# Weight loads in pieces, column norms, and a denser interleave in an attention and top-1 MoE kernel

## The chip, the core and the metric

The kernel runs on one core of a Trainium2 chip. A core has five engines that each run their own list of instructions in order: PE (TensorE: matmuls and transposes), DVE (VectorE), ACT (ScalarE), POOL (GpSimd) and SP (SyncE, which here only issues transfers); 16 DMA engines move the data. The metric is the device time of one execution in microseconds (us).

## The reference

Attention over columns, for each of 4 batches of 5056 tokens with 256 channels, and then a mixture of 8 experts of which each of the 20224 tokens uses one:

```python
qn = q / (norm(q, axis=1) + 1e-6);  kn = k / (norm(k, axis=1) + 1e-6)
s = softmax(kn.T @ qn / tau)              # 256 x 256 for each batch
x = v @ s                                 # 5056 x 256 for each batch
e = argmax(x @ w_gate)                    # one expert for each token
g = softmax(x @ w_gate)[e] * sigmoid((x @ w_output_gate)[e])
out[token] = g * (relu(x[token] @ w1[e]) @ w2[e])     # w1 256x1024, w2 1024x256
```

## The kernel before, in words

**Stages.** `gram(b)` makes s for one batch: 20 steps, each with two token rows for each of the 128 partitions, load q and k (SP, tile qk, 6 buffers), square them on ACT (L353), add the squares up on DVE (L354) and multiply on PE (s_ps, L366). Then come the norms: `both` is the sum of squares, PE adds it over the partitions with a matrix of ones (L381 for the norms of q, as a row that stands on every partition; L383 for those of k, as columns), ACT takes the root (L389), DVE does one Newton step and the reciprocal (L390 to L397) and scales s (L401). Softmax, a transpose and the product with the gate weights follow.

`mix(b)` makes x for one batch. It has 5 groups of 1024 tokens; in a group, 4 steps load v (SP, L465), transpose it on PE (vt_ps, L477), split it into a rounded part and a rest (vh on ACT L481, vl on DVE L483) and multiply (x_ps, L506 to L508); ACT copies x into the group's tile `st` (L509). After a group, `route` finds each token's expert on DVE (r_oh, L556), counts on PE (r_ps, L576) and has POOL scatter the tokens to DRAM by expert (xs_d, L598), eight transfers a group.

`blocks` runs the experts in units of 256 or 128 tokens: `fetch_w` has POOL fetch the unit's weights by an index (wbuf, L825), `fetch_x` has SP load its tokens (xg, L843), `prepare` splits these into two f16 parts (xr, ACT L880 and DVE L881) and has SP issue transposing transfers (xt, L885), `h_part` and `y_part` are the matmuls (L919 to L921, L942 to L944), `store` has POOL scatter the result (L954). A token load waits for a **mark**: a small POOL transfer (L615) behind the scatters of the tokens in question.

`prep` and `split` turn an expert's f32 weights into two f16 parts for the ranks 0 to 7 (experts in the order of their token counts so far): two loads of 1 MB (raw, L273 and L276) from the row that a table `ri` gives (SP reads it at L268), two Squares each on ACT for the scale (L297), a sum on PE (w_ps, L301), scaled copies (whi on ACT L310, wlo on DVE L311), and two writes to DRAM (wsc, L316). Rank 0 goes straight into wbuf. The raw of rank 1 lies in the `raw` buffers, that of the ranks above in `st` buffers, which the routing uses too.

**What sets the order.** The functions are generators, and the driver at the end takes steps of them in turn: Gram 0; mix(0) and mix(1) with the Grams 1 to 3 at GRATE (1.3) Gram steps to a mixing step; checkpoint 0 (the ranks); mix(2) with what is left of Gram 3, with the weights of rank 0 at PRATE, and from step OPEN on with the first units of `blocks`; checkpoint 1; mix(3) with blocks at BRATE and the weights of ranks 1 to 7 at MRATE; checkpoint 2; the other blocks with the remaining weights at WRATE. `pause(n)` gives n steps away. A scheduler orders each engine's list within that; each engine then runs its list in order and waits where its operands are late.

## Time and profile before

| | |
|---|---|
| median of 3 runs | 1206.93 us (1206.85 to 1208.63) |
| the profiled execution | 1209.88 us, its span in the trace 1208.1 us |
| mean granted PE clock | 0.990 |
| PE busy | 1174.4 us, 97% of the span |
| DVE, ACT, POOL busy | 748.5, 602.3, 517.9 us |
| mean DMA rate | 173 GB/s |

The profiled execution is one run, 2.95 us above the median. Times in rows of the trace are counted from the start of the span. Gram 0 and the first loads fill about the first 60 us; mix(2) runs to about 300 us, mix(3) to about 420, the units alone from there on. PE matmuls are pipelined: the duration of one is longer than the spacing to the next. Of an f32 matmul with a moving tile of 256 or 1 columns the trace has two records.

### The profile page before, as it was taken

To read this page: it belongs to the slowest core of one execution; us is meant where nothing else is said; L and a number is where in the kernel's file an instruction comes from. 1 tells how busy PE (TensorE), PEld (TensorE's weight loads), DVE (VectorE), ACT (ScalarE), POOL (GpSimd) and SP (SyncE) were. 2 spreads that over 40 slices of the span, in tenths; PEclk is the share of its full clock that TensorE was granted. 3 is DMA by queue.
4 is the path that set the end of the run, shared out by engine and by line. 5 is a ranking of instruction groups with operands and counts; after the bars stand their busy time and mean duration, and the time that the engine had idled before them with its cause. 6 is when DMAs were issued, how large, how long until landed. Compare 5 with 4: busy or idle time off the path is not lost.

```text
span 1208.1 us, 28097 instructions
## 1 busy us (share of the span) xinstructions
PE 1174.4 (97%) x10412; PEld 1066.4 (88%) x10412; DVE 748.5 (62%) x2300; ACT 602.3 (50%) x1193; POOL 517.9 (43%) x518
## 2 busy tenths in 40 slices
PE   8999999997997999999999999999999999999997
PEld 7899999887996888888888888888889999999997
DVE  7787768788685966566666654555554555555531
ACT  6576656576574555555556443333333444344432
POOL 0003756536565753333444433344444444444433
PEclk9999999998998999999999999999999999999999
DMA  9976888877767898657554436643325534336533
GB/s 319 330 246 207 301 277 259 295 242 215 212 242 236 223 264 178 150 147 174 148 137 126 112 80 113 182 76 77 72 63 176 112 73 82 79 81 197 168 104 130
DMA packets 186307, 208.56 MB, mean 173 GB/s; under 512 B 121832, under 2 KB 134510, under 8 KB 182200
## 3 DMA queue, kind: packets, MB, share of 16 engines
q1 hardware_dynamic: 145368, 139.41, 42.0%
q0 software_dynamic: 40512, 67.05, 18.9%
q8 instruction: 84, 1.38, 0.5%
q14 instruction: 55, 0.45, 0.1%
q10 hardware_dynamic: 288, 0.26, 0.1%
HBM read 281.84 MB, written 61.41 MB: 284 GB/s over the span
## 4 chain that ended last, share of the span: by engine, by line
PE 87%; DMA 6%; DVE 2%; issue 2%; ACT 1%; SPq 1%; POOL 0%; POOLq 0%; DVEq 0%; ACTq 0%
PE h_ps L919 11%; PE h_ps L921 11%; PE h_ps L920 11%; PE y_ps L942 11%; PE y_ps L943 11%; PE y_ps L944 11%; PE s_ps L366 10%; PE x_ps L506 3%; PE x_ps L508 2%; PE x_ps L507 2%; PE vt_ps L477 2%; DMA wbuf<-wsc,wi 1%; DMA qk<-in_k_dram 1%; DMA raw<-in_moe_w_dram 1%; DMA qk<-in_q_dram 1%
## 5 line engine op out<-in xcount | busy, mean ns | idle before, releaser
L924 DVE SCALAR_TENSOR_TENSOR hb<-h_ps,hb 128x512 f16<-128x512 f32 (+1 forms) x360 | 228.5, 636 | 276.0 <-ACT hb L923 275.1
L923 ACT ACTIVATE hb<-h_ps 128x512 f16<-128x512 f32 (+1 forms) x360 | 197.9, 552 | 364.1 <-PE h_ps L921 362.5
L919 PE MATMUL h_ps<-xt,wbuf 128*128 128x256 f16 (+1 forms) x1440 | 366.5, 262 | 3.0 <-ACT st L509 3.0
L921 PE MATMUL h_ps<-xt,wbuf 128*128 128x256 f16 (+1 forms) x1440 | 366.6, 262 | 0.0
L920 PE MATMUL h_ps<-xt,wbuf 128*128 128x256 f16 (+1 forms) x1440 | 366.5, 262 | 0.0
L942 PE MATMUL y_ps<-wbuf,hb 128*128 128x256 f16 x1296 | 353.3, 273 | 5.0 <-ACT yo L948 2.4
L944 PE MATMUL y_ps<-wbuf,hb 128*128 128x256 f16 x1296 | 353.3, 273 | 0.0
L943 PE MATMUL y_ps<-wbuf,hb 128*128 128x256 f16 x1296 | 353.3, 273 | 0.0
L825 POOL DMA_INDIRECT wbuf<-wsc,wi x172 | 177.8, 1034 | 404.5 <-PE h_ps L921 365.2
L598 POOL DMA_INDIRECT xs_d<-st,r_si x160 | 168.1, 1051 | 199.2 <-DVE r_d L550 101.9
L954 POOL DMA_INDIRECT out_dram<-yo,b_id x162 | 165.4, 1021 | 69.2 <-issue 42.3
L366 PE MATMUL s_ps<-qk 128*128 128x256 f32 x640 | 152.4, 390 | 5.8 <-DMA qk<-in_q_dram 3.9
L920 PEld LDWEIGHTS <-wbuf 128*128 128x128 f16 x1440 | 141.0, 98 | 16.9 <-issue 3.2
L919 PEld LDWEIGHTS <-wbuf 128*128 128x128 f16 x1440 | 142.1, 99 | 14.1
L921 PEld LDWEIGHTS <-wbuf 128*128 128x128 f16 x1440 | 141.1, 98 | 13.3
L943 PEld LDWEIGHTS <-hb 128*128 128x128 f16 x1296 | 126.8, 98 | 19.3 <-issue 5.6
L366 PEld LDWEIGHTS s_ps<-qk 128*128 128x128 f32 x640 | 121.4, 196 | 21.2 <-DMA qk<-in_k_dram 3.9
L944 PEld LDWEIGHTS <-hb 128*128 128x128 f16 x1296 | 126.8, 98 | 14.9
L942 PEld LDWEIGHTS <-hb 128*128 128x128 f16 x1296 | 126.8, 98 | 14.3
L354 DVE TENSOR_TENSOR acc<-acc,sq 128x1024 f32<-128x1024 f32 x76 | 92.9, 1223 | 46.8 <-ACT sq L353 45.4
L880 ACT ACTIVATE xr<-xg,b_sx 128x256 f16<-128x256 f32 x162 | 74.6, 502 | 66.8 <-DVE b_sx L233 46.4
L353 ACT ACTIVATE sq<-qk 128x1024 f32<-128x1024 f32 x76 | 80.3, 1060 | 53.0 <-DMA qk<-in_k_dram 44.8
(191 smaller groups left out, 1448.8 us busy)
## 6 DMA issues: line engine op xcount, KB each, us to landing
xg<-xs_d SPq DMA_DIRECT2D x72, 272.0 KB
qk<-in_q_dram SPq DMA_DIRECT2D x75, 256.0 KB
qk<-in_k_dram SPq DMA_DIRECT2D x75, 256.0 KB
v<-in_v_dram SPq DMA_DIRECT2D x32, 512.0 KB
raw<-in_moe_w_dram SPq DMA_DIRECT2D x16, 1024.0 KB
wsc<-whi SPq DMA_DIRECT2D x14, 512.0 KB
wsc<-wlo SPq DMA_DIRECT2D x14, 512.0 KB
v<-in_v_dram SPq DMA_DIRECT2D x8, 480.0 KB
```

The lines of the kernel that those rows point to most:

```text
L366: nc.tensor.matmul(s_ps[:, c, :], kt[:, 1, t, c * P : (c + 1) * P], qt[:, 0, t, :], start=st == 0 and t0 == 0 and t == 0 and c == 0 and n ...
L598: ins = nc.gpsimd.indirect_dma_start(out=xs_d[:, :], out_offset=bass.IndirectOffsetOnAxis(ap=si[:np_, t : t + 1], axis=0), in_=st[:np_, t, ...
L825: nc.gpsimd.indirect_dma_start(out=wbuf[half][:, at_of(u), :], out_offset=None, in_=wsc[half][:end, :], in_offset=bass.IndirectOffsetOnAxi ...
L919: nc.tensor.matmul(hp, w1s[:, 0, c, fs], xh, start=fi == 0 and c == 0, stop=False, **KWM)
L920: nc.tensor.matmul(hp, w1s[:, 0, c, fs], xl, start=False, stop=False, **KWM)
L921: nc.tensor.matmul(hp, w1s[:, 1, c, fs], xh, start=False, stop=fin, **KWM)
L923: nc.scalar.activation(hh, h_ps[:, :, :w], AF.Relu)
L924: nc.vector.scalar_tensor_tensor(out=hb[:, 1, 2 * fp : 2 * fp + 2, :w], in0=h_ps[:, :, :w], scalar=0.0, in1=hh, op0=ALU.max, op1=ALU.subtract,
L942: nc.tensor.matmul(y_ps[:, t, :], hb[:, 0, f, tsl], w2s[:, 0, f, :], start=st, stop=False, **KWM)
L943: nc.tensor.matmul(y_ps[:, t, :], hb[:, 0, f, tsl], w2s[:, 1, f, :], start=False, stop=False, **KWM)
L944: nc.tensor.matmul(y_ps[:, t, :], hb[:, 1, f, tsl], w2s[:, 0, f, :], start=False, stop=fin, **KWM)
L954: ins = nc.gpsimd.indirect_dma_start(out=out[:, :], out_offset=bass.IndirectOffsetOnAxis(ap=un["id"][:, t : t + 1], axis=0), in_=un["yo"][ ...
```

## The change

The raw weights are loaded in two halves each, and from rank 2 on into buffers of the tile `v` instead of `st`; each half of the two f16 parts is written to DRAM as soon as it is made, in pieces of 256 KB instead of 512 KB. The norms of q and k are both taken as columns (four matmuls with one column of ones, 128x4 values), with the inverse root on DVE by a shift of the exponent and two Newton steps and a correction, all on 128x4; for q the result is put on the diagonals of two 128x128 matrices (dq), and a further matmul with ones (n_ps) makes the row on every partition; s is scaled from there. ACT's root goes. The Gram rate in mix(0) and mix(1) is 1.45. The preparation of weights has other rates and pauses, its part in mix(3) is cut after rank 1, the blocks open two mixing steps sooner (OPEN 8), and token loads are looked for in every step of a unit.

```diff
-    GRATE = 1.3
-    PRATE = 1.2
-    DEEP, LAG, REST = 2, 3, 2
-    LATE, OPEN, MARKED = 5, 10, 3
+    GRATE, AHEAD_RATE = 1.3, 1.45
+    PRATE = 1.5
+    DEEP, LAG, REST, SLOW = 2, 4, 1, 4
+    LATE, OPEN, MARKED = 5, 8, 3
     FAR, NEAR = 5, 1
     BRATE = 0.7
     DRY = 4
-    MRATE = 1.2
-    WRATE = 0.8
+    MRATE = 1.6
+    WRATE = 1.0
...
-                raw = wk.tile([P, R, CW], F32, tag="st", name=f"raw{r}_{half}", bufs=STB)
-                raw = raw.rearrange("p r w -> p (r w)")[:, :HW1]
+                parts = [
+                    ld.tile([P, 4, C], F32, tag="v", name=f"raw{r}_{half}_{i}", bufs=VB).rearrange("p t c -> p (t c)")
+                    for i in range(2)
+                ]
             else:
                 raw = big.tile([P, HW1], F32, tag="raw", name=f"raw{r}_{half}", bufs=3)
+                parts = [raw[:, i * HW1 // 2 : (i + 1) * HW1 // 2] for i in range(2)]
+            raws.append(parts)
...
+            rows = wraw[half][bass.ds(row, P), :]
+            for i, part in enumerate(parts):
+                if half == 0:
+                    nc.sync.dma_start(part, rows[:, i * HW1 // 2 : (i + 1) * HW1 // 2])
+                else:
+                    nf = FC // 2
+                    of = rows.rearrange("(f a) (b d) -> (a b) f d", f=FC, d=C)[:, i * nf : (i + 1) * nf, :]
+                    nc.sync.dma_start(part.rearrange("p (f d) -> p f d", f=nf), of)
+                yield
...
-                gather()
-                yield
-            yield from pause(LAG if n == 0 else REST)
+                yield from gather()
+            yield from pause(LAG if n == 0 else SLOW if r > AHEAD + 1 else REST)
...
+            for n, part in enumerate((hi, lo)):
+                nc.sync.dma_start(wsc[half][rows, n * HW1 + a.start : n * HW1 + a.stop], part[:, a])
             yield
-        for n, part in enumerate((hi, lo)):
-            nc.sync.dma_start(wsc[half][rows, n * HW1 : (n + 1) * HW1], part)
...
-        nc.tensor.matmul(k_ps[:, :C], onesf, both[:, 0, :], start=True, stop=True, skip_group_check=True)
+        for i in range(2):
+            for c in range(CC):
+                n = i * CC + c
+                nc.tensor.matmul(
+                    k_ps[:, n : n + 1], both[:, i, c * P : (c + 1) * P], onesf[:, 0:1],
+                    start=n == 0, stop=n == 2 * CC - 1, skip_group_check=True,
+                )
...
+        ss, hss, half, y = t4("n_ss"), t4("n_hss"), t4("n_half", I32), t4("n_y")
+        nc.vector.tensor_scalar(out=ss, in0=k_ps[:, : 2 * CC], scalar1=1e-36, scalar2=None, op0=ALU.max)
+        nc.vector.tensor_scalar(
+            out=half, in0=ss.bitcast(I32), scalar1=1, scalar2=None, op0=ALU.logical_shift_right
+        )
+        nc.vector.tensor_scalar(
+            out=y.bitcast(I32), in0=half, scalar1=-1.0, scalar2=float(RSQRT), op0=ALU.mult, op1=ALU.add
+        )
+        nc.vector.tensor_scalar(out=hss, in0=ss, scalar1=-0.5, scalar2=None, op0=ALU.mult)
+        for _ in range(2):
+            t = t4("n_t")
+            nc.vector.tensor_tensor(out=t, in0=hss, in1=y, op=ALU.mult)
+            nc.vector.tensor_tensor(out=t, in0=t, in1=y, op=ALU.mult)
+            nc.vector.scalar_tensor_tensor(out=y, in0=t, scalar=1.5, in1=y, op0=ALU.add, op1=ALU.mult)
+        r, e = t4("n_r"), t4("n_t")
+        nc.vector.tensor_tensor(out=r, in0=ss, in1=y, op=ALU.mult)
+        nc.vector.tensor_tensor(out=e, in0=r, in1=r, op=ALU.mult)
+        nc.vector.tensor_tensor(out=e, in0=ss, in1=e, op=ALU.subtract)
+        nc.vector.scalar_tensor_tensor(out=e, in0=e, scalar=0.5, in1=y, op0=ALU.mult, op1=ALU.mult)
+        nc.vector.scalar_tensor_tensor(out=r, in0=e, scalar=1e-6, in1=r, op0=ALU.add, op1=ALU.add)
+        nc.vector.tensor_scalar(out=r[:, CC:], in0=r[:, CC:], scalar1=tau_b, scalar2=None, op0=ALU.mult)
+        nc.vector.reciprocal(r, r)
+        dq = one.tile([P, CC, P], F32, tag="root", name=f"dq{b}")
         for c in range(CC):
-            nc.tensor.matmul(
-                k_ps[:, C + c : C + c + 1], both[:, 1, c * P : (c + 1) * P], onesf[:, 0:1],
-                start=False, stop=c == CC - 1, skip_group_check=True,
-            )
-        ss = k_ps[:, : C + CC]
-        root = one.tile([P, C + CC], F32, tag="root", name=f"root{b}")
-        nc.scalar.activation(root, ss, AF.Sqrt)
-        nc.vector.tensor_scalar(out=root, in0=root, scalar1=1e-30, scalar2=None, op0=ALU.max)
-        r = one.tile([P, C + CC], F32, tag="rq", name=f"rn{b}")
-        nc.vector.reciprocal(r, root)
-        nc.vector.tensor_tensor(out=r, in0=ss, in1=r, op=ALU.mult)
-        nc.vector.tensor_tensor(out=r, in0=r, in1=root, op=ALU.add)
-        nc.vector.tensor_scalar(out=r, in0=r, scalar1=0.5, scalar2=1e-6, op0=ALU.mult, op1=ALU.add)
-        nc.vector.tensor_scalar(out=r[:, C:], in0=r[:, C:], scalar1=tau_b, scalar2=None, op0=ALU.mult)
-        nc.vector.reciprocal(r, r)
-        yield from pause(HOLD)
-        rq, rk = r[:, :C], r[:, C:]
+            nc.vector.tensor_scalar(out=dq[:, c, :], in0=ident, scalar1=r[:, c : c + 1], scalar2=None, op0=ALU.mult)
+        yield from pause(HOLD + 1)
+        n_ps = ps_x.tile([P, 512], F32, tag="x", name=f"n_ps{b}")
+        nc.tensor.matmul(n_ps[:, :C], onesf, dq.rearrange("p c m -> p (c m)"), start=True, stop=True)
+        yield
+        rq, rk = n_ps[:, :C], r[:, CC:]
...
+                adv("x", fetch_x, got["prep"] + QKB)
...
-        _beside(mix(b) if b else first, (ahead, GRATE))
+        _beside(mix(b) if b else first, (ahead, AHEAD_RATE))
...
-    preps = prep(AHEAD, E)
+    preps = chain(prep(AHEAD, AHEAD + 1), pause(12), prep(AHEAD + 1, E))
```

How this moves the instructions is seen in three places. In the rows, a number behind a name tells tiles of one name apart, and xN counts neighbours that are alike. The first place is ACT around the start of mix(2)'s second group, where the weights of rank 0 (tiles raw_0 and raw_1) are squared; sq are the Gram's squares, st_0 and st_1 the first two groups' tiles. Before:

```order
L353 ACTIVATE sq_15_0_3168<-qk_15_3165 128x1024
L509 COPY st_0_2766<-x_ps 128x272
L481 CAST vh<-vt_ps 128x512
L509 COPY st_1_2954<-x_ps 128x272 x2
L297 ACTIVATE wbuf_155,wss<-raw_0_2793 128x1024 x2
L559 ACTIVATE r_d<-r_d 128x64
L481 CAST vh<-vt_ps 128x512
L567 ACTIVATE r_og_2936<-r_og_2936 128x8
L509 COPY st_1_2954<-x_ps 128x272 x2
L297 ACTIVATE wbuf_156,wss<-raw_1_2833 128x1024 x2
L481 CAST vh<-vt_ps 128x512
L353 ACTIVATE sq_16_0_3246<-qk_16_3243 128x1024
```

And now:

```order
L359 ACTIVATE sq_19_0_3245<-qk_19_3238 128x1024
L537 COPY st_0_2889<-x_ps 128x272 x2
L509 CAST vh<-vt_ps 128x512
L537 COPY st_0_2889<-x_ps 128x272
L304 ACTIVATE wbuf_155,wss<-raw_0_2916 128x1024
L537 COPY st_0_2889<-x_ps 128x272
L304 ACTIVATE wbuf_155,wss<-raw_0_2916 128x1024
L587 ACTIVATE r_d<-r_d 128x64
L304 ACTIVATE wbuf_156,wss<-raw_1_2957 128x1024
L509 CAST vh<-vt_ps 128x512
L595 ACTIVATE r_og_3061<-r_og_3061 128x8
L537 COPY st_1_3079<-x_ps 128x272
```

The Squares of the weights stood as two pairs ahead of the last four steps of Gram 3 (sq_16 is the first of them); now all Gram steps stand before them, and they stand singly between copies of x, vh and the routing.

The second place is the norms of Gram 3, in mix(2). On DVE now, from the first reading of the sums (wbuf is the split of rank 0's weights, r_ names belong to the routing):

```order
L399 TENSOR_SCALAR n_ss_3363<-k_ps_3358 128x4
L582 TENSOR_REDUCE r_mv<-r_val 128x8
L400 TENSOR_SCALAR n_half_3365<-n_ss_3363 128x4
L317 SCALAR_TENSOR_TENSOR wbuf_155<-raw_0_2916,wsw,wbuf_155 128x1024
L584 TENSOR_TENSOR r_oh<-r_val,r_mv 128x64
L406 TENSOR_SCALAR n_hss_3364<-n_ss_3363 128x4
L403 TENSOR_SCALAR n_y_3366<-n_half_3365 128x4
L317 SCALAR_TENSOR_TENSOR wbuf_155<-raw_0_2916,wsw,wbuf_155 128x1024
L592 TENSOR_TENSOR r_os<-st_1_3079,r_oh 128x64
L511 TENSOR_TENSOR vl<-vt_ps,vh 128x512
L409 TENSOR_TENSOR n_t_3371<-n_hss_3364,n_y_3366 128x4
```

and the chain's end, with the diagonals and the scaling of s:

```order
L417 SCALAR_TENSOR_TENSOR n_r_3379<-n_t_3380,n_r_3379 128x4
L418 TENSOR_SCALAR n_r_3379<-n_r_3379,tau_b 128x2
L597 SCALAR_TENSOR_TENSOR r_gt<-r_og_3564,r_se 128x8
L419 RECIPROCAL n_r_3379<-n_r_3379 128x4
L598 RECIPROCAL st_2_3333<-r_gt 128x8
L422 TENSOR_SCALAR dq_3388<-ident,n_r_3379 128x128 x2
L429 SCALAR_TENSOR_TENSOR s_sb_3252<-s_sb_3252,n_r_3379,n_ps_3533 128x256 x2
```

On PE now, between the sums (k_ps) and the new matmul (n_ps), with the alike rows of the mixing left out:

```order
L390 MATMUL k_ps_3358<-onesf,both_3356 128x1 x4
L534 MATMUL x_ps<-ah_2442,vh 128x272
...
L505 MATMUL vt_ps<-ident,v_3_0_3448 128x128 x4
L505 MATMUL vt_ps<-ident,v_3_2_3571 128x128 x4
...
L604 MATMUL r_ps<-r_oh,tri 128x64
...
L505 MATMUL vt_ps<-ident,v_3_2_3571 128x128 x4
L505 MATMUL vt_ps<-ident,v_4_0_3671 128x128 x4
L425 MATMUL n_ps_3533<-dq_3388,onesf 128x256
L308 MATMUL w_ps<-wss,onesf 128x2
L534 MATMUL x_ps<-ah_2442,vh 128x272
```

Before, the norms of q came from one matmul of 256 columns, and there was no second one:

```order
L508 MATMUL x_ps<-ah_2498,vl 128x272
L381 MATMUL k_ps_3521<-both_3519,onesf 128x256
L383 MATMUL k_ps_3521<-onesf,both_3519 128x1 x2
L301 MATMUL w_ps<-wss,onesf 128x2
L477 MATMUL vt_ps<-ident,v_4_0_3546 128x128 x4
L477 MATMUL vt_ps<-ident,v_4_2_3688 128x128 x4
L506 MATMUL x_ps<-ah_2498,vh 128x272
```

Between k_ps and n_ps PE has 36 x matmuls (12 rows of each of the lines 534 to 536), 16 transposes and one group of r_ps; n_ps stands ahead of w_ps and the next x matmuls. On DVE 50 rows lie between n_ss and the scaling of s, of which 17 are the chain's small operations, 4 vl, 2 weight splits and 2 dq.

The third place is ACT in mix(3), where unit 4, the first behind the second mark, is prepared (xr; st_1 and st_2 are groups of mix(3), the pieces of raw_0 and raw_1 belong to rank 1). Before:

```order
L481 CAST vh<-vt_ps 128x512
L509 COPY st_2_4619<-x_ps 128x272 x3
L880 ACTIVATE xr_3657<-xg,b_sx 128x256 x2
L509 COPY st_2_4619<-x_ps 128x272
L297 ACTIVATE whi_1_4850,wss<-raw_1_4164 128x1024 x2
L880 ACTIVATE xr_3657<-xg,b_sx 128x256 x2
L923 ACTIVATE hb<-h_ps 128x512
```

And now:

```order
L537 COPY st_1_4451<-x_ps 128x272
L587 ACTIVATE r_d<-r_d 128x64
L537 COPY st_1_4451<-x_ps 128x272
L595 ACTIVATE r_og_4433<-r_og_4433 128x8
L509 CAST vh<-vt_ps 128x512
L908 ACTIVATE xr_3663<-xg,b_sx 128x256 x2
L537 COPY st_1_4451<-x_ps 128x272
L908 ACTIVATE xr_3663<-xg,b_sx 128x256 x2
L537 COPY st_1_4451<-x_ps 128x272
```

It stood in the middle of group st_2; now it stands after the second copy of group st_1.

More of the change, by code (lines that the diff above doesn't have):

```diff
@@ L24 @@
 EXP_MASK = 0x7F800000
+RSQRT = 0x5F3759DF
 def _beside(main, *others):
@@ L271, in gather @@
             )
-            if half == 0:
-                nc.sync.dma_start(raw, wraw[0][bass.ds(row, P), :])
-            else:
-                rows = wraw[1][bass.ds(row, P), :].rearrange("(f a) (b d) -> (a b) f d", f=FC, d=C)
-                nc.sync.dma_start(raw.rearrange("p (f d) -> p f d", f=FC), rows)
-            raws.append(raw)
+            rows = wraw[half][bass.ds(row, P), :]
[7 more added lines that the diff above has]
+                yield
         for n, (r, half) in enumerate(jobs):
             while len(raws) < min(n + DEEP, len(jobs)):
-                gather()
-                yield
-            yield from pause(LAG if n == 0 else REST)
+                yield from gather()
+            yield from pause(LAG if n == 0 else SLOW if r > AHEAD + 1 else REST)
             yield from split(raws[n], half, r)
@@ L296, in split @@
             a = slice(i * HW1 // 2, (i + 1) * HW1 // 2)
-            nc.scalar.activation(hi[:, a], raw[:, a], AF.Square, accum_out=ss[:, i : i + 1])
+            nc.scalar.activation(hi[:, a], raw[i], AF.Square, accum_out=ss[:, i : i + 1])
             yield
@@ L305, in split @@
         root2(tot, KW, sw, invw[:, half, r : r + 1])
-        src, dh, dl = raw, hi, lo
-        cuts = [(slice(None), slice(i * HW1 // 2, (i + 1) * HW1 // 2)) for i in range(2)]
-        for i, a in enumerate(cuts):
-            nc.scalar.activation(dh[a], src[a], AF.Copy, scale=sw)
+        for i in range(2):
+            a = slice(i * HW1 // 2, (i + 1) * HW1 // 2)
+            nc.scalar.activation(hi[:, a], raw[i], AF.Copy, scale=sw)
             nc.vector.scalar_tensor_tensor(
-                out=dl[a], in0=src[a], scalar=sw, in1=dh[a], op0=ALU.mult, op1=ALU.subtract
+                out=lo[:, a], in0=raw[i], scalar=sw, in1=hi[:, a], op0=ALU.mult, op1=ALU.subtract
             )
+            for n, part in enumerate((hi, lo)):
+                nc.sync.dma_start(wsc[half][rows, n * HW1 + a.start : n * HW1 + a.stop], part[:, a])
             yield
-        for n, part in enumerate((hi, lo)):
-            nc.sync.dma_start(wsc[half][rows, n * HW1 : (n + 1) * HW1], part)
         if half == 1:
@@ L397, in gram, with t4 @@
-        nc.vector.reciprocal(r, r)
-        yield from pause(HOLD)
-        rq, rk = r[:, :C], r[:, C:]
+        for i in range(2):
+            for c in range(CC):
[4 more added lines that the diff above has]
+                )
+        def t4(tag, dt=F32):
+            return sm.tile([P, 2 * CC], dt, tag=tag, name=f"{tag}{b}")
```

## The prediction

> **What bounds the kernel now.** I read first the page's busy shares and the chain that ended last.
>
> ```profile
> PE 1174.4 (97%) x10412; PEld 1066.4 (88%) x10412; DVE 748.5 (62%) x2300; ACT 602.3 (50%) x1193; POOL 517.9 (43%) x518
> PE 87%; DMA 6%; DVE 2%; issue 2%; ACT 1%; SPq 1%; POOL 0%; POOLq 0%; DVEq 0%; ACTq 0%
> ```
>
> TensorE is the bound; an edit can win only what PE loses. So next the stretches (length, then busy time of PE, PEld, DVE, ACT, POOL, then granted clock, DMA share, GB/s), to find where it loses.
>
> ```profile
> 60.00:150.00 90.00, 90.00 (x630) 84.44 (x630) 69.30 (x168) 63.76 (x128) 33.70 (x32) 1.00 0.77 251
> 210.00:300.00 90.00, 78.75 (x561) 73.27 (x560) 70.71 (x268) 56.44 (x126) 44.37 (x46) 0.94 0.80 253
> 360.00:390.00 30.00, 22.44 (x176) 19.92 (x176) 17.00 (x74) 15.05 (x34) 16.04 (x17) 0.89 0.81 247
> 450.00:750.00 300.00, 300.00 (x2757) 269.11 (x2756) 183.94 (x521) 151.17 (x283) 119.25 (x115) 1.00 0.57 138
> 369.30:372.70 3.40, 2.93 (x12) 2.75 (x13) 0.87 (x5) 0.51 (x1) 1.58 (x2) 0.50 1.10 201
> sum 17.00, PE 14.53 PEld 13.01 DVE 7.14 ACT 8.22 POOL 7.64; mean PE 3.63 PEld 3.25 DVE 1.79 ACT 2.06 POOL 1.91
> ```
>
> PE is idle 11.25 us in 210:300 and 7.56 in 360:390, and 1.6 at a weight fetch (the last wait below): 20.4. The last two rows are of the stretches in which the clock stood at 0.50 (four, behind these stops, 17.0 us in all; one is shown, and the sum): 14.53 us of busy time at half clock, of which half, 7.3, is lost. Together **27.7 us** lie in reach. What PE waited for from 200 to 430 us (in total, times, longest):
>
> ```profile
> PE r_ps L576 <- DVE r_oh L556: 5.3, 1, 5.3
> PE r_ps L576 <- ACT st L509: 4.1, 1, 4.1
> PE h_ps L919 <- ACT st L509: 3.0, 1, 3.0
> PE y_ps L942 <- ACT yo L948: 2.4, 1, 2.4
> PE vt_ps L477 <- DVE vl L483: 2.1, 1, 2.1
> PE y_ps L942 <- DMA wbuf<-wsc,wi: 1.6, 1, 1.6
> ```
>
> Each goes back to one cause on another engine. The 4.1 (at 239 us): ACT, in order, stood at the first Square of the first expert's weights; SP had not issued their load sooner because it waited for the table row of the expert.
>
> ```profile
> 239.59 1.06 ACT L297 ACTIVATE wbuf<-raw 128x1024 f16<-128x1024 f32 x1 [7.00 <-DMA raw<-in_moe_w_dram]
> SPq L268 <- DVE tb_ni L666: 6.0, 1, 6.0
> ```
>
> The 5.3 (at 284): DVE's backlog behind the norm chain of the last Gram matrix. PE's norm matmuls, ACT's table load for the root, and DVE (start, length):
>
> ```profile
> 271.43 0.59 PE L381 MATMUL k_ps<-both,onesf 128*128 128x256 f32 x2
> 271.86 0.50 PE L383 MATMUL k_ps<-onesf,both 128*128 128x1 f32 x4
> 272.22 0.36 PE L301 MATMUL w_ps<-wss,onesf 128*128 128x2 f32 x2
> 272.44 1.07 PE L477 MATMUL vt_ps<-ident,v 128*128 128x128 f32 x8
> ...
> 272.74 1.28 ACT L389 ACT_TABLE_LOAD   x1
> ...
> 276.05 1.76 DVE L392 RECIPROCAL rn<-root 128x258 f32<-128x258 f32 x1
> 284.78 1.75 DVE L397 RECIPROCAL rn<-rn 128x258 f32<-128x258 f32 x1
> 288.66 0.20 DVE L561 TENSOR_REDUCE r_se<-r_d 128x8 f32<-128x64 f32 x1
> 288.79 0.21 DVE L556 TENSOR_TENSOR r_oh<-r_val,r_mv 128x64 bf16<-128x64 f32 x1
> ```
>
> From the sums (272.2) to the second reciprocal's end (286.5) go 14.3 us; r_oh, behind it, starts at 288.79. The 3.0, 2.4 and 2.1 (367 to 380): SP stood at a raw load whose buffer, a routing tile, had to be scattered first, and behind it stood the transposes that ACT's xr tiles needed.
>
> ```profile
> SPq L276 <- DMA xs_d<-st,r_si: 18.5, 2, 9.4
> 360.39 9.85 SPq L885 DMA_TRANSPOSE xt<-xr  x4
> 371.62 0.51 ACT L880 ACTIVATE xr<-xg,b_sx 128x256 f16<-128x256 f32 x1 [7.06 <-DMA xt<-xr]
> ```
>
> **Part by part.** *Gram rate 1.45.* The last Gram steps come before the first expert's load, and ACT's Squares of that load are parted by st and vh copies, so the table row and the load have some two groups' PE work as cover. The 4.1 and its clock go; left I take 1 (0 to 4, the whole old stop; SP still can't load before the table row). The denser Gram loads in mix(0) and mix(1) meet DMA engines at 0.77 where PE was 90.00 of 90: nothing, up to 2, none below.
>
> *Norms in columns.* Prices from the groups (busy, mean ns), and the spacing of x matmuls from two neighbours:
>
> ```profile
> L392 DVE RECIPROCAL rn<-root 128x258 f32<-128x258 f32 x4 | 7.0, 1762 | 0.1
> L394 DVE TENSOR_TENSOR rn<-rn,root 128x258 f32<-128x258 f32 x4 | 1.7, 418 | 0.0
> L396 DVE TENSOR_SCALAR rn<-rn,tau_b 128x2 f32<-128x2 f32 x4 | 1.1, 275 | 0.0
> L483 DVE TENSOR_TENSOR vl<-vt_ps,vh 128x512 fp32r<-128x512 f32 x80 | 54.3, 685 | 12.9 <-PE x_ps L508 4.2 <-ACT vh L481 3.6 <-PE h_ps L921 2.8
> L311 DVE SCALAR_TENSOR_TENSOR wbuf<-raw,wsw,wbuf 128x1024 f16<-128x1024 f32 x4 | 5.1, 1276 | 0.0
> L354 DVE TENSOR_TENSOR acc<-acc,sq 128x1024 f32<-128x1024 f32 x76 | 92.9, 1223 | 46.8 <-ACT sq L353 45.4
> L366 PE MATMUL s_ps<-qk 128*128 128x256 f32 x640 | 152.4, 390 | 5.8 <-DMA qk<-in_q_dram 3.9 <-ACT s_sb L375 1.9
> 283.37 0.29 PE L507 MATMUL x_ps<-al,vh 128*128 128x272 f32 x1
> 283.49 0.29 PE L508 MATMUL x_ps<-ah,vl 128*128 128x272 f32 x1
> ```
>
> Removed per Gram: two reciprocals at 1.76, two wide products at 0.42, three further DVE operations (0.3 each by the row of L396), the root and two table loads (one before it, one back) at 1.28 on ACT. Added: 17 small DVE operations, two 128x128 ones, and four column matmuls plus one 128x256 for one 128x256 and two columns. A small operation is worth between its spacing (288.66 to 288.79: 0.13) and the 0.275 of L396: 2.2 to 4.7 us for 5.3; I take 0.13, since neighbours of other chains fill its tail. [...]
>
> PE: four column records took 272.22 - 271.86 = 0.36, so 0.09 each, two to a matmul; two more columns cost 0.36 a Gram, 1.1 for the three beside mixing (up to 2.7 by 0.23 a record).
>
> The new matmul n_ps is a wait that was not there: PE, in order, stands at it until DVE has the diagonals, and behind it stand w_ps and mixing. In mix(2), DVE has 50 operations between the first reading of k_ps and dq: 4 vl at 0.6, 2 weight splits at 1.25, some 43 small at 0.13, two dq at 0.2, so 11.0 us; PE has between k_ps and n_ps 36 x matmuls at 0.125 (the pair above), 16 transposes at 0.11 (eight end within 1.07) and a group of r_ps, 6.5. So PE waits 4.5, and 5 with the handovers (from 0, if DVE's operations overlap more than I reckon, to 7, if each of the 17 takes 0.145 more, 2.5); its half clock costs 1.7 (half of a 3.4 us stretch; 0 to 3.4, two stretches). [...] In mix(0) DVE has 4 vl, two dq and 32 small operations there, 7.0, and in mix(1) 2 vl, two dq and 33 small, 5.9. PE has 24 x matmuls, 18 transposes and 16 s_ps matmuls at 2 x 0.238 (152.4 over 640), 12.6, and 36, 16 and 12, 12.0: covered by 5.6 and 6.1, nothing.
>
> *Raw in pieces, in the v buffers; mix(3) preps as 1, pause, 2 to 7.* The raw of rank 2 no longer waits for a scatter, and its loads stand behind the first transposes on SP: the 7.56 and its clock go. What is late next is unit 4, now prepared at the first copies of mix(3)'s second group. It needs the second mark, and a read of its rows behind that.
>
> ```profile
> 299.90 0.19 PE L576 MATMUL r_ps<-r_oh,tri 128*128 128x64 bf16 x1
> 314.14 0.99 POOL L598 DMA_INDIRECT xs_d<-st,r_si  x1 [0.31 <-issue]
> 319.63 0.59 POOL L615 DMA_DIRECT2D mark<-xs_d  x1 [4.50 <-DMA xs_d<-st,r_si]
> ```
>
> The mark goes 19.7 us after the last r_ps, and a transfer takes up to 5.5 us to be seen (314.14 to 319.63), so mark and rows are there 25 to 31 us after it; PE has up to those copies 60 x matmuls at 0.125, 36 of h_ps, 39 of y_ps and 22 transposes at 0.11 (300.00 over 2757 records), 18.3 us. The gap is 7 to 13 for ACT; PE loses less, since it can work ahead of a stuck ACT until its PSUM tiles are full (some 4 us: four x tiles at 0.75 and a y tile). I take 3 (0 to 8). Rank 1's raw now comes before its Square with less lead: 1 (0 to 4, half of rank 0's 7.00 at most). Smaller wsc writes and 44 more issues go beside PE work.
>
> *The weights of unit 7* are fetched by POOL behind scatters as before, and a step sooner needed: the 1.6 becomes 3 (1.6 to 5.5, the longest transfer above).
>
> *Ranks 2 to 7 at WRATE 1.0, rows fetched a step sooner:* in 450:750 PE is 300.00 of 300 with DVE at 61% and ACT at 50%. Nothing; if one fetch is late, another 1.6.
>
> Sum: 27.7 go; 1 + 5 + 1.7 + 1.1 + 3 + 1 + 3 = 15.8 come: 11.9 less. The profiled execution took 1209.88 us (span 1208.1), 2.95 above the median 1206.93; 1209.88 - 11.9 = 1198.0, and by the same 2.95 a median of **1195.0**.
>
> **Rivals.** *DVE becomes the bound at n_ps in all three Grams (slower).* In mix(0) and mix(1) the cover holds only if DVE is about level with PE when k_ps is done. Between the sum `both`, on which k_ps waits, and n_ss DVE has 4 sums of squares at 1.22, 5 vl and 15 small operations (9.9), and 5, 5 and 14 (10.9). If all of that is still ahead, and the 17 take those 2.5 more, the waits are 9.9 + 7.0 + 2.5 - 12.6 = 6.8 and 10.9 + 5.9 + 2.5 - 12.0 = 7.3, with 1.7 each of clock 17.5; with mix(2) at 7 + 3.4, 3.7 more: 21.2, and 1216.2. It begins to cost once DVE is 3 us behind at k_ps (5.6 less 2.5), and the gain of 11.9 is gone at some three fifths of it. For it: DVE is busy 69.30 of 90 there. Against: its sums waited 45.4 us for ACT's Squares in this kernel (row of L354), so its backlog is not its own.
>
> *The second mark and SP give it back (no change).* Unit 4's wait at 8, both raw waits at 4, the weight fetch at 5.5: 5 + 3 + 3 + 2.5 = 13.5 more, 1208.5. For it: the mark's chain is longer than the work ahead of it. Against: PE can run on mix(3)'s other tiles.
>
> *All waits hidden.* Lower ends throughout: 1.1 + 1.6 = 2.7 come, 25.0 go: 1181.9. It needs DVE to finish dq in 6.5 us.
>
> *The change doesn't do what it says:* for the order of ACT, PE and SP that is excluded, since it is written into the program; it is left for when transfers land, which the second rival prices.
>
> **How the numbers follow.** Forecast 0.50 (1188 to 1202), all hidden 0.15, second mark and SP 0.20 (1202 to 1209), DVE 0.15 (1202 to 1216, by how far behind it is). The range 1183 to 1209 leaves out the ends of the first and last, some 2 in 10. What a measurement can tell from no change is 0.2%, 2.4 us: 1204.5 to 1209.3. Faster: 0.50 + 0.15 + half of 0.20 + 0.01 of DVE's = 0.76; same: the other 0.10 and 0.02; slower: DVE's other 0.12.
>
> **What would show it.** Right: no 7 us ACT wait at the first expert's raw; no table loads at the norms; PE waiting some 5 us at n_ps once, in mix(2), and not in mix(0) and mix(1); SP not stuck at raw behind scatters; PE idle in 210:300 about 6, in 300:450 about 8. Wrong: several n_ps waits (first rival), a wait at xr or h_ps of over 6 us near 320 to 340 (second), or PE losing time behind 450 us, where I cost the faster preps at nothing.

## The result: 1.0% slower, where 1.0% faster was forecast

The changed kernel takes 1221.71 us in the median of 6 runs (1216.67 to 1223.33). The kernel before, run again beside it, takes 1207.78 (6 runs, 1206.85 to 1210.55). The measured ratio is 1.0104 (95% interval 1.0089 to 1.012), some 12.5 us slower; by the two medians it is 13.9 us. The forecast was 1195.0 with a range of 1183 to 1209; sign and range are both wrong.

The profiled execution of after took 1217.96 us, with a span of 1216.3 and a mean granted PE clock of 0.989. It lies 3.75 us below the median. Against the profiled execution of before (1209.88) it is 8.1 us longer, and only this part of the loss can be read from the two traces. The rest lies in executions of which no trace is there, and stays open; the four slower ones had a mean granted clock of 0.986 to 0.987, which points to more half clock in them.

The experiments further down ran on chips on which before took 4 to 6% longer than here (1259.7 to 1274.0 us) and after 5% (1277.15 and 1283.70), so each of them is compared with before in its own set alone. The first letter of a label is the set: e ran on one chip, f on a second, g, h and i on a third. On that third chip before took 1263.37, 1259.70 and 1272.83 us in the three sets, so times of different sets can't be compared even there.

### The profile after

The page's busy shares and the chain that ended last:

```profile
PE 1178.6 (97%) x10428; PEld 1069.1 (88%) x10428; DVE 734.9 (60%) x2348; ACT 592.6 (49%) x1181; POOL 523.8 (43%) x518
PE 80%; DMA 7%; issue 5%; DVE 3%; POOL 2%; ACT 2%; SPq 0%; POOLq 0%; ACTq 0%; DVEq 0%
```

PE's share of that chain fell from 87% to 80%. DVE is busy 13.6 us less and ACT 9.7 less, as the lighter norms should make them, and the kernel is slower: neither was the bound. Of the 8.2 us that the span grew, 4.0 are idle time of PE (1216.3 - 1178.6 = 37.7, against 33.7) and 4.2 are longer busy time. From 60 to 450 us half clock costs 9.6 us against 7.3, reckoned as half of the 19.13 and 14.53 us that PE is busy in such stretches (from 274.70 us after has 17 matmuls in 3.41 us at 0.50, and in the next 3.42 us, at 1.00, 30). Before has one more such stretch, at the end of Gram 0, which after doesn't have:

```profile
41.60:45.00 3.40, 1.47 (x10) 1.28 (x9) 1.23 (x1) 1.70 (x3) 0.00 (x0) 1.00 1.01 377
45.00:48.40 3.40, 3.40 (x10) 2.68 (x9) 2.06 (x3) 3.13 (x4) 0.00 (x0) 0.50 1.05 396
```

PE's stop there, behind ACT's copy of s, is 1.18 us in after and 1.94 in before. The change doesn't decide whether a stretch follows: on the chips of the experiments after has it (f1, granted clock 0.94 from 30 to 60 us) and before doesn't (h1, 1.00). Over the whole span half clock is 9.6 against 9.0 us; what else makes PE's busy time longer, some 3.6 us, is not traced to its lines here (the new n_ps rows alone are 2.6).

Where PE loses it, by stretches (length, then busy time of PE, PEld, DVE, ACT, POOL, then granted clock, DMA share, GB/s); the last three rows are of stretches at half clock, and "sum" is over all of them, 23.8 us:

```profile
210.00:300.00 90.00, 81.18 (x599) 76.18 (x598) 65.57 (x276) 53.41 (x119) 53.27 (x49) 0.96 0.81 252
300.00:390.00 90.00, 82.62 (x701) 75.02 (x699) 62.06 (x253) 50.47 (x115) 48.95 (x50) 0.94 0.78 235
390.00:450.00 60.00, 53.08 (x481) 46.92 (x479) 39.57 (x160) 26.43 (x51) 39.03 (x38) 0.94 0.60 166
450.00:750.00 300.00, 300.00 (x2758) 269.05 (x2756) 185.25 (x536) 154.60 (x287) 117.03 (x113) 1.00 0.57 148
...
366.90:373.70 6.80, 5.86 (x34) 5.07 (x35) 3.70 (x14) 4.30 (x10) 1.54 (x2) 0.50 0.65 228
418.10:424.90 6.80, 3.06 (x16) 2.28 (x17) 0.07 (x1) 0.23 (x1) 5.27 (x6) 0.50 0.55 205
sum 23.80, PE 19.13 PEld 16.66 DVE 11.42 ACT 10.62 POOL 11.16; mean PE 3.83 PEld 3.33 DVE 2.28 ACT 2.12 POOL 2.23
```

For the two later stretches, the same view of before:

```profile
300.00:390.00 90.00, 82.22 (x719) 75.62 (x718) 60.72 (x260) 52.17 (x119) 49.89 (x50) 0.96 0.74 230
390.00:450.00 60.00, 58.36 (x544) 52.22 (x542) 47.99 (x176) 31.45 (x57) 39.20 (x38) 1.00 0.91 238
```

From 210 to 300 PE is idle 8.8 us (11.25 before; the forecast was about 6), from 300 to 390 7.4 (7.8) and from 390 to 450 6.9 (1.6; the forecast for these two was about 8): 23.1 together, and with half of the 19.13 busy at half clock 32.7. The forecast had 27.7 going down to 15.8. Behind 450 us PE is at 300.00 of 300, as forecast. What PE waited for from 60 to 450 us (in total, times, longest):

```profile
PE x_ps L534 <- ACT st L537: 10.9, 3, 4.8
PE h_ps L947 <- DMA wbuf<-wsc,wi: 6.9, 1, 6.9
PE n_ps L425 <- DVE dq L422: 4.0, 1, 4.0
PE y_ps L970 <- DVE vl L511: 1.0, 1, 1.0
PE vt_ps L505 <- DVE vl L511: 0.5, 1, 0.5
```

The three causes of before (r_ps behind ACT's Squares, r_ps behind r_oh, h_ps and y_ps in mix(3)) no longer stand in the list by name. In their place stand x matmuls that wait for ACT's copies, three times. What ACT, SP and POOL did at these places, and one row of PE (start, length, engine, what it did, in brackets the idle time before it and what ended it):

```profile
247.13 0.60 POOL L643 DMA_DIRECT2D mark<-xs_d  x1 [5.06 <-DMA xs_d<-st,r_si]
249.22 3.63 SPq L871 DMA_DIRECT2D xg<-xs_d  x4
255.08 0.91 ACT L908 ACTIVATE xr<-xg,b_sx 128x256 f16<-128x256 f32 x2 [7.28 <-DVE b_ix L237]
...
312.44 1.06 ACT L304 ACTIVATE whi<-raw 128x1024 f16<-128x1024 f32 x1 [6.12 <-DMA raw<-in_moe_w_dram]
329.53 0.91 ACT L908 ACTIVATE xr<-xg,b_sx 128x256 f16<-128x256 f32 x2 [2.57 <-DVE b_sx L234]
...
342.69 1.37 SPq L321 DMA_DIRECT2D wsc<-whi  x2
347.65 1.59 SPq L321 DMA_DIRECT2D wsc<-wlo  x2
351.12 0.34 SPq L280 DMA_DIRECT2D raw<-in_moe_w_dram  x1
353.83 0.29 PE L536 MATMUL x_ps<-ah,vl 128*128 128x272 f32 x1
354.15 7.72 SPq L913 DMA_TRANSPOSE xt<-xr  x4
363.93 0.51 ACT L908 ACTIVATE xr<-xg,b_sx 128x256 f16<-128x256 f32 x1 [3.96 <-DMA xt<-xr]
...
371.85 1.04 POOL L853 DMA_INDIRECT wbuf<-wsc,wi  x1 [6.93 <-DMA wsc<-wlo]
...
414.17 1.00 POOL L626 DMA_INDIRECT xs_d<-st,r_si  x1 [0.30 <-DMA xs_d<-st,r_si]
418.07 1.05 POOL L853 DMA_INDIRECT wbuf<-wsc,wi  x1 [0.30 <-DMA xs_d<-void,tb_ei]
```

Four places carry the loss:

- **252.8 us, 4.8 of PE.** ACT stands at unit 0's xr, the first token work. Its rows lie behind mark 0, which POOL issued at 247.13, after 5.06 us in which it waited for the scatters to land; SP issued the load at 249.22, and the xr began at 255.08. Behind it in ACT's list stood copies of x into `st`, which free PE's x tiles. In before the same xr ran at 259.74 without such a wait: it stood later in ACT's list, and mark 0 had gone out at 242.07, 5.1 us sooner.
- **312.1 us, 2.3 of PE.** ACT waited 6.12 us for a raw piece of rank 1.
- **364.0 us, 3.8 of PE.** ACT waited 3.96 us at the next unit's xr, until 363.93, for the first of four transposes, which SP had issued at 354.15. In front of them SP had wsc writes (342.69, 347.65) and a raw load (351.12), but it was through with these at 351.46. It stood another 2.7 us at a semaphore of PE, which moved as the x matmul of 353.83 ended (354.12). By the kernel, xt takes a buffer of the tag `vl`, which these matmuls read. From the issue to ACT's release went 9.8 us; in before, for the transposes that cost PE its stop there, 11.2 (360.39 to 371.62). A transpose issued at 278.24 in after landed 2.5 us later. What made the late ones slow isn't shown.
- **414.9 us, 6.9 of PE.** POOL issued a weight fetch at 418.07, behind eight scatters, the last of them at 414.17, and two transfers of empty rows. POOL was late as a whole: it had stood 6.93 us, until 371.85, for a wsc write to land, and from there to 418.07 its longest pause was 1.55 us.

### The profile page after: what moved, and what is told of

It is laid out like the page before. It is cut to its first block, busy times and chain, and to the rows that moved or that the text cites. A ratio compares the mean times of both kernels' runs of the same rounds, so it can differ in the third digit from the quotient of the medians.

```text
span 1216.3 us, 28282 instructions
## 1 busy us (share of the span) xinstructions
PE 1178.6 (97%) x10428; PEld 1069.1 (88%) x10428; DVE 734.9 (60%) x2348; ACT 592.6 (49%) x1181; POOL 523.8 (43%) x518
## 4 chain that ended last, share of the span: by engine, by line
PE 80%; DMA 7%; issue 5%; DVE 3%; POOL 2%; ACT 2%; SPq 0%; POOLq 0%; ACTq 0%; DVEq 0%
PE h_ps L947 10%; PE h_ps L949 10%; PE h_ps L948 10%; PE y_ps L970 10%; PE y_ps L971 10%; PE y_ps L972 10%; PE s_ps L372 9%; PE x_ps L534 3%; PE x_ps L536 2%; PE x_ps L535 2%; DMA qk<-in_k_dram 2%; PE vt_ps L505 2%; DMA wbuf<-wsc,wi 2%; DMA xt<-xr 1%; POOL out_dram L982 1%
## 5 line engine op out<-in xcount | busy, mean ns | idle before, releaser
L626 POOL DMA_INDIRECT xs_d<-st,r_si x160 | 173.3, 1083 | 187.7 <-DVE n_y L411 93.1
L372 PE MATMUL s_ps<-qk 128*128 128x256 f32 x640 | 148.6, 384 | 5.0 <-DMA qk<-in_q_dram 3.8
L534 PE MATMUL x_ps<-ah,vh 128*128 128x272 f32 x320 | 103.5, 326 | 11.3 <-ACT st L537 10.9
```

What stands on the lines that cost most here:

```text
L372: nc.tensor.matmul(s_ps[:, c, :], kt[:, 1, t, c * P : (c + 1) * P], qt[:, 0, t, :], start=st == 0 and t0 == 0 and t == 0 and c == 0 and n ...
L626: ins = nc.gpsimd.indirect_dma_start(out=xs_d[:, :], out_offset=bass.IndirectOffsetOnAxis(ap=si[:np_, t : t + 1], axis=0), in_=st[:np_, t, ...
```

## The experiments

Theories, as they stood after the two traces. **A**: the time is lost at unit 0's token work, which now stands ahead of mark 0 on ACT; either the Gram rate (A1) or the early opening (A2) put it there. **B**, a rival: the column norms cost more than the one wait that is seen. **C**, a rival: the pieces and the other rates of the preparation are what costs. **D**, a rival that the later runs were made for: the stops hide one another, and a stop that is taken away is replaced by the next one. All medians are in us, and each ratio is the measured one, to before in the same set; it differs a little from the quotient of the two medians (1.0032 for h1).

| label | kernel | median | before | ratio (95%) |
|---|---|---|---|---|
| h1_before | before itself | 1263.71 | 1259.70 | 1.0009 (0.9978 to 1.0040) |
| f1_after | after | 1283.70 | 1273.97 | 1.0072 (1.0036 to 1.0108) |
| g1_after | after | 1277.15 | 1263.37 | 1.0103 (1.0071 to 1.0135) |
| e1_b_rate145 | before, rate 1.45 | 1280.14 | 1262.52 | 1.0149 (1.0090 to 1.0208) |
| g4_b_rate145 | the same | 1272.09 | 1263.37 | 1.0074 (1.0047 to 1.0100) |
| e2_b_norm | before, column norms | 1272.41 | 1262.52 | 1.0077 (1.0052 to 1.0103) |
| f2_b_norm | the same | 1272.59 | 1273.97 | 0.9994 (0.9961 to 1.0026) |
| g3_b_norm | the same | 1272.58 | 1263.37 | 1.0051 (1.0017 to 1.0086) |
| h2_b_pieces | before, pieces and prep rates | 1268.47 | 1259.70 | 1.0065 (1.0039 to 1.0092) |
| h3_b_open8 | before, early opening | 1274.89 | 1259.70 | 1.0094 (1.0045 to 1.0144) |
| e3_a_rate13 | after, rate 1.3 | 1277.43 | 1262.52 | 1.0148 (1.0088 to 1.0207) |
| f4_a_rate13 | the same | 1286.18 | 1273.97 | 1.0086 (1.0060 to 1.0112) |
| e4_a_open10 | after, OPEN 10 | 1275.14 | 1262.52 | 1.0125 (1.0068 to 1.0182) |
| i2_open10 | the same | 1282.88 | 1272.83 | 1.0085 (1.0053 to 1.0118) |
| f3_a_oldnorm | after, old norms | 1290.14 | 1273.97 | 1.0114 (1.0073 to 1.0155) |
| h4_a_r13_o10 | after, rate 1.3, OPEN 10 | 1275.70 | 1259.70 | 1.0135 (1.0105 to 1.0164) |
| g2_xrlate | after, unit 0 held back | 1273.27 | 1263.37 | 1.0076 (1.0041 to 1.0110) |
| i1_xrl_o10 | held back, OPEN 10 | 1279.41 | 1272.83 | 1.0082 (1.0045 to 1.0118) |

**The scale.** Before against itself and after on two of these chips.

> The kernel before itself, for a trace from the chip of the runs beside it: no change, within 0.3%. If this chip's engines too lose time at many places from 90 to 480 us, the raw stop (ACT 7.0), the r_oh stop (5.3) and the transposes (ACT 7.1) are still there, each within 3 us of what the first trace shows, and what else is lost lies in pieces of 0.3 to 1.3 us.

> The changed kernel again, on the chip of the runs beside it. It is the base for them: 1.0 to 1.2% above the kernel before, with the stops at xr for mark 0 (4.8), n_ps (4.0), raw of rank 1 (2.3), xr behind the transposes (3.8) and the weight fetch (6.9).

> The changed kernel as the base of the runs beside it: 0.7 to 1.1% above the kernel before.

Before against itself gives 1.0009, so the method finds no difference where there is none, to some 0.3%. After is 0.7% and 1.0% slower here, the same sign as in the result.

**The Gram rate alone.**

```diff
-        _beside(mix(b) if b else first, (ahead, GRATE))
+        _beside(mix(b) if b else first, (ahead, 1.45))
```

> The kernel before, with only the Gram rate in mix(0) and mix(1) at 1.45. Rate theory (the rate alone brings unit 0's token work on ACT ahead of mark 0's rows): the 4.1 us stop at the first expert's raw goes, a stop of 4 to 6 us at x_ps behind ACT's xr near 250 us takes its place with its half clock, the 5.3 us stop behind the norm chain stays; 1205 to 1210 us, no change. Opening theory (OPEN 8 is what brings the token work ahead of the mark): no such stop, only the raw stop goes; 1200 to 1203.

> The kernel before with only the Gram rate at 1.45. Rate theory: the stop at xr for mark 0 stands here too (4 to 5 us and its clock) in place of the raw stop, the norm stop stays: 0 to 0.6% slower than the kernel before. On a chip whose engines lose time at many places it was 1.5% slower. If the rate is harmless: 0.3 to 0.5% faster.

It costs 1.5% and 0.7%. ACT's waits from 200 to 300 us in the two:

```profile
ACT xr L880 <- DVE b_ix L236: 6.2, 1, 6.2
ACT wbuf L297 <- DMA raw<-in_moe_w_dram: 5.2, 1, 5.2
```

```profile
ACT xr L880 <- DVE b_ix L236: 5.7, 1, 5.7
ACT wbuf L297 <- DMA raw<-in_moe_w_dram: 4.3, 1, 4.3
```

The xr wait of after is there with this one number changed, with OPEN still at 10. The wait at the raw of rank 0, which the rate was priced to remove, is there as well. On g4's chip before itself has only 2.0 us of it, in two parts (h1), so the rate took nothing away there.

**The opening and the rate, each taken back in after.** The first diff is that of e4 and i2, the second that of e3 and f4:

```diff
-    LATE, OPEN, MARKED = 5, 8, 3
+    LATE, OPEN, MARKED = 5, 10, 3
```

```diff
-    GRATE, AHEAD_RATE = 1.3, 1.45
+    GRATE, AHEAD_RATE = 1.3, 1.3
```

> The changed kernel with the first units opened at step 10 as before. Opening theory (the early opening makes unit 4 and the fetches meet marks, SP's queue and POOL's scatters too early): the stops from 310 to 425 us (2.3, 1.0, 3.8, 6.9 and some 6 of clock) shrink by half or more, 1208 to 1215, and by the strong form the stop at xr for mark 0 goes as well, 1203 to 1208. Rate theory: the stop at xr for mark 0 stays at 4 to 5 us whatever OPEN is.

> The changed kernel with OPEN 10, once more, beside the run with the work held back. The xr wait for mark 0 stays at 7 us on ACT; 1.0 to 1.4% above the kernel before as on the other chip, 0.3 to 0.6% above the run beside it.

> The changed kernel with the Gram rate back at 1.3. Rate theory: no stop at xr for mark 0 (4.8 and 1.7 of clock less), the raw stop of 4.1 may come back in part, n_ps waits shift; the stops from 310 to 425 us stay as they were; 1210 to 1219, 3 to 9 below the changed kernel. Opening theory: the stop at xr stays, within 2 of the changed kernel.

> The changed kernel with the Gram rate at 1.3, once more, beside the changed kernel. Rate theory: 3 to 9 us faster than the changed kernel, xr of unit 0 no longer waits for mark 0. If the rate isn't the cause: within 3.

ACT's waits in e4, and then in i2:

```profile
ACT xr L908 <- DVE b_ix L237: 7.2, 1, 7.2
```

```profile
ACT xr L908 <- DVE b_ix L237: 7.1, 1, 7.1
```

With OPEN 10 the xr wait stays at 7 us, with rate 1.3 no such row is left in either run. So A2 falls as the cause of this wait, and A1 holds: the denser Gram steps run out a group sooner, and the units' first steps take their place. How long the wait is varies: after itself has 7.5 us of it in f1 and 1.4 in g1. And e3 and f4 have lost it and are not shown to be faster for it: f4 has 1.0086 beside f1's 1.0072 on the same chip. So this wait alone is not shown to be what separates after from before.

**Unit 0 held back.** Instead of the rate, only the order is changed: unit 0's xr stands behind ACT's last copy of mix(2)'s second group, and its DVE work behind a vl of the third.

```diff
+    HELD = 7
...
+            if b == SOON and j == HELD:
+                held.extend(x.ins for x in left)
...
+        if u == 0:
+            with tc.issue_after(held[0]), tc.issue_after(held[1]):
+                prepare_now(u)
```

> The changed kernel with one thing held back: ACT's and DVE's work on unit 0's tokens is ordered behind the first copies of mix(2)'s third group, where the kernel before had it; everything else is left. Mark theory (this work, brought ahead of mark 0's rows, costs the 4.8 us stop and 1.7 of clock): no x_ps stop near 253 us, 4 to 8 us faster than the changed kernel. Rival (the time is lost later anyway, since the units are then later): the stop goes, less than 2 us faster.

> The changed kernel with unit 0's work on ACT and DVE held back to where the kernel before has it, and OPEN 10. If the early token work and the early opening carry the loss: no xr wait for mark 0, no wait for rank 1's raw, 0.4 to 1.0% below the changed kernel, about equal to the kernel before. Rival (each stop taken away is replaced by the next of ACT's, SP's and POOL's rows): still 0.5 to 1.0% above the kernel before.

i1 has OPEN 10 besides. The xr wait is gone in both. g2 is 0.3% better than g1 by the medians, with intervals that overlap; but g1's own trace has only 1.4 us of the xr wait, so there was little to take away. i1 equals i2 (1.0082 and 1.0085). PE's waits from 200 to 330 us, in i2 and then in i1:

```profile
PE x_ps L534 <- ACT st L537: 14.0, 7, 4.3
PE n_ps L425 <- DVE dq L422: 6.2, 1, 6.2
```

```profile
PE n_ps L426 <- DVE dq L423: 6.7, 1, 6.7
PE x_ps L536 <- ACT st L539: 6.3, 4, 2.9
```

Holding back takes 7.7 us of x_ps waits (14.0 to 6.3) away in this stretch, 0.6% of the time. PE's busy time in the same stretch, in i2 and then in i1:

```profile
200.00:330.00 130.00, 107.97 (x739) 100.22 (x738) 82.01 (x328) 68.10 (x157) 70.09 (x64) 0.91 0.71 222
```

```profile
200.00:330.00 130.00, 110.06 (x765) 102.03 (x762) 82.55 (x331) 69.67 (x160) 71.31 (x66) 0.91 0.70 223
```

Of the 7.7 us only 2.1 became busy time in this stretch (107.97 to 110.06); the rest went to other stops, 0.5 more at n_ps, 1.6 at r_ps behind ACT and smaller ones. That is what D expects, but the pair can't show it. The profiled execution of i1 is the fastest of its seven (1273.47), that of i2 the slowest of its four (1284.31); the two lie 10.8 us apart, and from 60 to 480 us PE is busy 8.2 us longer in i1 (366.15 against 357.91), more than the wait that was taken away. A gain of 0.3% or so, 0.27% by the medians of i1 and i2, is neither shown nor excluded by the ratios.

**The norms alone, and taken back in after.** Before gets L387 to L431 of after:

```diff
-        root = one.tile([P, C + CC], F32, tag="root", name=f"root{b}")
-        nc.scalar.activation(root, ss, AF.Sqrt)
...
+        dq = one.tile([P, CC, P], F32, tag="root", name=f"dq{b}")
...
+        nc.tensor.matmul(n_ps[:, :C], onesf, dq.rearrange("p c m -> p (c m)"), start=True, stop=True)
```

> The kernel before, with only the norms in columns. If the columns are good by themselves: the stop of 5.3 (with 1.0 and 0.5 ahead of it and 3.4 of clock, 10 us) goes, an n_ps wait of up to 4 with 1.7 of clock comes, in mix(0) and mix(1) none; 1199 to 1204. If the n_ps wait eats the gain (rival): waits at n_ps of 8 us or more in all; 1205 to 1210.

> The kernel before with only the norms in columns, once more, beside the changed kernel. On the first chip, whose engines all lose 0.3 to 1 us at many places from 90 to 480 us, it was 0.8% slower. If that holds for chips without these losses (columns cost: n_ps waits plus what PE adds): 0.3 to 0.8% slower. If the columns are good by themselves and the first chip hid it: 0.3 to 0.7% faster, one n_ps wait of 4 to 6 us in mix(2) for the 5.3 stop and its clock.

> The kernel before with only the norms in columns: 0.8% slower and equal on two chips whose engines lose time at many places. Where they don't: one n_ps wait of 4 to 6 us, the raw stop of 4.1 and the late stops of the kernel before kept or moved; 0.1 to 0.5% faster than the kernel before. If the columns cost more than they bring: 0.2 to 0.8% slower.

f3 is the reverse edit, old norms in after.

> The changed kernel with the old norms (a row of 258, root on ACT). Columns-cost theory: faster than the changed kernel by 3 to 8 us, with no n_ps wait. Order theory (the loss comes from what stands in ACT's, SP's and POOL's rows ahead of marks, transposes and fetches): the stop at xr for mark 0 stays 4 to 5 us, the late stops stay, the norm chain's r_oh stop returns; within 4 of the changed kernel.

PE's waits in e2, and then in e3, where mix(2)'s wait is longest:

```profile
PE n_ps L420 <- DVE dq L417: 4.4, 1, 4.4
```

```profile
PE n_ps L425 <- DVE dq L422: 6.8, 1, 6.8
```

Every kernel with column norms whose wait is attributed has it once, at 3.4 to 6.8 us, and never in mix(0) or mix(1). Alone the norms give 1.0077, 0.9994 and 1.0051: a gain of them is not shown, and in two of the three sets they make before slower. But after with the old norms is at 1.0114 beside 1.0072, so taking them out of after wins nothing, and B falls as the main cause.

**The pieces alone, the opening alone, norms and pieces.** h2 is after with the old norms, rate 1.3 and OPEN 10, so that the pieces, the v buffers and the preparation's rates are left. h4 is after with rate 1.3 and OPEN 10 (norms and pieces). h3 is before with this edit, the second number being the rate that goes with the opening:

```diff
-    LATE, OPEN, MARKED = 5, 10, 3
+    LATE, OPEN, MARKED = 5, 8, 3
...
-    MRATE = 1.2
+    MRATE = 1.6
```

> The changed kernel without three of its parts: old norms, Gram rate 1.3, OPEN 10; what is left is the raw in pieces and v buffers, the quarter writes, the preparation's rates and pauses and the extra token loads. Opening theory for the late stops: with OPEN 10 these parts cost nothing or win the 360 to 390 stop; 0.6% faster to 0.2% slower than the kernel before. Rival (SP's longer row of pieces is what holds the transposes and costs): 0.4 to 1.2% slower.

> The kernel before with OPEN 8 and, since unit 4 needs rank 1's weights sooner, MRATE 1.6. Opening theory: rank 1's raw is waited for (5 us on ACT), the transposes and fetches are late; 0.4 to 1.0% slower. Rival (opening is harmless): within 0.3%.

> The changed kernel with Gram rate 1.3 and OPEN 10: norms in columns and the pieces. If rate and opening carry the loss: from 0.5% faster to equal to the kernel before, no xr stop for mark 0, no wait for rank 1's raw, n_ps one wait of 4 to 7. If the columns and the pieces carry it: 0.5 to 1.2% slower.

The stretch from 360 to 510 us in h1 (before), and then in h3:

```profile
360.00:510.00 150.00, 129.72 (x1042) 110.25 (x1040) 91.05 (x355) 68.19 (x141) 76.22 (x74) 0.89 0.69 208
```

```profile
360.00:510.00 150.00, 118.95 (x947) 98.72 (x945) 87.01 (x346) 69.69 (x144) 71.06 (x70) 0.89 0.58 165
```

The early opening brings units forward, and PE runs dry behind them: 118.95 us busy of 150, against 129.72, so 10.8 less. From 60 to 360 us PE is busy 2.7 us more in h3, so 8.1 us are lost up to 510; the two executions differ by 8.3 (1274.89 and 1266.55). The pieces alone cost 0.65%, norms with pieces 1.35%; C is a part, like the others.

**What follows from all of them.** Taken singly, the rate costs 0.7 to 1.5%, the norms -0.1 to 0.8%, the pieces 0.65%, the opening (with its MRATE) 0.9%. Added up, from the lowest to the highest, that is 2.3 to 3.9%, and all together cost 0.7 to 1.0%. On the third chip alone it is 2.8% (g4, g3, h2, h3) against 1.0% (g1). So the parts don't add up, and taking one of them back beside after (f3, f4, g2) gave nothing that the intervals can tell from after; e3, e4 and i2 had no after beside them. This fits D, but no pair of traces shows a stop being replaced by another. How much of after's loss belongs to which part on the first chip is not settled, since no single part ran there. No version was found that is faster than before.

## Why the prediction was wrong, step by step

| term | forecast, us | the trace of after |
|---|---|---|
| raw of rank 0 | 1 | no PE stop |
| n_ps in mix(2), its clock | 5 + 1.7 | 4.0 + 1.7 |
| PE's norm matmuls, for three Grams | 1.1 | some 1.3 (in Gram 0 the columns take 0.95, as row and columns had taken 0.94, and n_ps 0.43 to the next matmul) |
| n_ps in mix(0), mix(1) | 0 | 0 |
| the second mark, at unit 4 | 3 | ACT waits 2.57, no PE stop |
| raw of rank 1 | 1 | 2.3 + 1.7 of clock |
| transposes in mix(3) | 0 | 3.8 + 2.9 |
| weight fetch | 3 | 6.9 + 1.5 |
| unit 0's token work behind mark 0 | not in the sum | 4.8 + 1.7 |
| end of Gram 0 | not in the sum | 0.8 less, and 1.7 of clock less in this execution |
| end of the program, behind PE's last matmul | 0 | 1.9 (7.7 against 5.8) |

**Right.** The wait at n_ps was placed and sized: once, in mix(2), 4.0 for 5. DVE took 9.9 us from n_ss (264.25) to the end of dq (274.13), against a forecast of 11.0. One row of the groups gives the price of a small operation (busy, mean ns):

```profile
L413 DVE TENSOR_TENSOR n_r<-n_ss,n_y 128x4 f32<-128x4 f32 x4 | 0.7, 167 | 0.1
```

The others lie at 0.15 to 0.17 us too, near the 0.13 taken and far from 0.275; only the one on 128x2 (L418) takes 0.25. The first rival, DVE as the bound at n_ps in all three Grams, needed waits that no run shows. The unit 4 term was too high, the denser Gram loads before 210 us cost little (PE 149.35 of 150 from 60 to 210 us), and the faster preparation behind 450 us costs nothing, all as priced or better.

**Wrong: "The last Gram steps come before the first expert's load [...]. The 4.1 and its clock go".** They went, on the first chip. The step looked at the Squares and the raw alone. The same rate moves everything that stood behind the Gram steps, and unit 0's xr, waiting on mark 0, came to stand ahead of copies that PE needs: 4.8 + 1.7 us, more than the 4.1 + 1.7 won. Only unit 4's move was priced. e1 and g4 show that the rate alone does this; in them the raw wait of rank 0 is there as well (5.2 and 4.3 us).

**Wrong: "its loads stand behind the first transposes on SP: the 7.56 and its clock go".** The load of a raw no longer waits for a scatter, but ACT again waited for transposes: 3.8 + 2.9 us. The step took SP's late issue for the whole stop and put two things at nothing. One is the time that these transposes need after their issue: 9.8 us in after, and 11.2 already in before, by the rows 360.39 and 371.62 of the prediction itself. The other is the buffer of xt, for which SP stood until PE's x matmuls were done with it, at 354.12. The writes and the load that stand ahead of the transposes were not what held them last; whether they would be late without them was not tried.

**Mis-sized.** The weight fetch, 3 with an upper end of 5.5, was 6.9 and its half clock. It was priced by one transfer, and what held it were the transfers in front of it on POOL, whose whole list was late by then: 6.93 us had gone, until 371.85, in waiting for a wsc write. f1 and g1 don't show this stop, so it is not in every execution. The raw of rank 1 came to 4.0 with its clock, the end of its range. Its cause isn't settled: the wait is there at 5.5 us on ACT in f1 and g1, is not seen in e4, i1 and i2, where OPEN is 10, but is 4.3 in h4, where OPEN is 10 too, and 1.0 at most in e3 and f4, where it is 8.

**Behind all of it: the sum itself.** Each stop was priced as if it could be taken out by itself, and its length won. The runs speak against that: f4 has lost an xr wait of 7.5 us and is not faster than f1, and four parts that cost 2.8% one by one cost 1.0% together. A likely reason, which was only argued, is that from 210 to 450 us ACT, SP and POOL work for two pipelines at once; a stop of PE lets them catch up, and without it the next late transfer is met sooner. The forecast's "all waits hidden" was the case with the least support, but its 27.7 us "in reach" were taken as if any part of them could be had alone.

**Open.** How the 12.5 us divide among the parts on the first chip, where no part ran alone; the 3.75 us between after's profiled execution and its median; what the pieces and the norms cost by themselves where nothing else disturbs; and which stop takes the place of which.
